# Attention ahead of the MLP with its output kept in DRAM, the last two MLP chunks side by side, and five experts in plain fp32

## Chip, cores and metric

One core of one Trainium2 chip. The metric is the device time of one execution in microseconds (us). Before the change three runs gave 1048.82, 1049.22 and 1049.54 us: a median of 1049.22 us.

## What is computed

Three layers, one after the other, over 4 x 576 = 2304 tokens of width 512. First causal attention with a decay (8 heads of width 64), then an MLP with a squared ReLU, then a layer in which each token goes to one of eight experts, each of which takes 288 tokens.

```python
scores = q @ k.T / 8 + (cum[:, None] - cum[None, :])      # cum = cumsum(log f), causal
x = softmax(scores) @ v                                   # -> (2304, 512)
x = relu(x @ w_in) ** 2 @ w_out                           # 512 -> 2048 -> 512
logits = x @ w_gate                                       # (2304, 8)
# all (token, expert) pairs by falling logit: a token takes the first expert that has room (288)
out[mask_e] = relu(x[mask_e] @ w1[e]) @ w2[e]             # 512 -> 1024 -> 512, e = 0..7
```

## The kernel before

**A recorded program and a planner.** The kernel calls `s.op(...)` for each small task, with the engines that could do it and a cost for each. `Sched.run` then places all tasks by list scheduling: an engine that is free takes the ready task with the lowest `s.base`, from its model of costs. The result is one fixed order for each engine (PE, DVE, ACT, POOL) and for SP, which issues the DMAs. On the chip every engine goes through its own order and stops at an instruction whose inputs are not there.

**Attention** (`attention`, `pair`) goes by batches `b` 0 to 3 and in each by four pairs of heads, 16 pairs in all. A pair has scores on PE (L496), a fused add and minimum on DVE (L513), the exponential on ACT (L520), transposes on PE (L552) with copies out of PSUM, the product with v (L569), and a normalizer: the row sums are transposed on PE (L607), written to DRAM, read back broadcast, and multiplied in (L624, L626). The result of a batch goes to SBUF tiles `xa` (two chunks of 256 tokens) and the first 64 tokens of each batch to `xrem`.

**The MLP** (`moe1_chunk`) goes by nine chunks of 256 tokens: two for each batch, and a last one of the four times 64 tokens in `xrem`. To keep fp32 accuracy at the faster matmul format, operands are split into a high and a low part of type fp32r, and each product is three matmuls. A chunk has 192 first-product matmuls of 256 columns (L692 to L694), then squared ReLU, a split into `hh` and `hl`, and 96 second-product matmuls of 512 columns (L716 to L718). Its 256 output rows go to DRAM (`x2d`), are transposed (L793) and give the logits (L801). The weights, which arrive as 64-bit words, are put together on DVE by three integer instructions for each piece (L656 to L658, 32 pieces) and split, on ACT and POOL above all. All of this is due (`s.base`) in the order: attention 0; weights 1; then for each batch `b` attention `b+1` (2 + 2b) and chunks of `b` (3 + 2b).

**The last chunk** has another form: `gate_weights` works out `w_out @ w_gate` on DVE beforehand (L819), so that the logits come from the hidden layer (L728, L729, then L747), and the second products, which only the gathers need, are due late (29), beside the routing.

**Routing and experts.** `phase(m)` settles which expert fills up next and with which tokens. It is a chain of small DVE instructions with PE between them: three rounds of a histogram (18 matmuls, L1023) with two small matmuls (L1028, L1038) each, then ranks and the list of token numbers (L1119). Phase 7 has no rounds. `expert(m)` then gathers 288 rows of `x2d` (POOL issues three indirect DMAs, L1151), transposes them on PE (L1218), splits them, and does 32 first products as three fp32r matmuls each (L1234 to L1236, 288 columns). The second products (32) are single plain fp32 matmuls (L1259) for experts 0 to 6, and split for expert 7 (L1262 to L1264). A plain matmul has two records in the trace. A split weight is loaded into a tile `wr`; its high part is a copy on ACT, its low part a subtraction on POOL (L1190), 8 pieces of 128 x 512 for each of the two weights. Transposes (L1275), copies, and three indirect DMAs of POOL (L1282) write the result.

```python
PLAIN = range(E - 1)                                                # L44
s.op(lo_alts(512, LOE(m, which, i, 0, c)), ... e.tensor_sub(lo ...  # L1190: POOL for m > 0
```

Of the kernel before, what the change touches and what calls it, by code (L numbers as in the profile page):

```python
# [8 lines left out]
F = mybir.dt.float32  # L9
# [21 lines left out]
XB0 = 1  # L31
RS = [("z", z) for z in (31, 30, 29)]
WS = [("z", 28)]
TM = 1
# [3 lines left out]
NSM = 4  # L38
HM = 50.0
# [4 lines left out]
PLAIN = range(E - 1)  # L44
# [322 lines left out]
class K:  # L367
# [75 lines left out]
    def att_pools(self):  # L443
        self.xp = self.pool("xp", ctx=self.main_es, side="right")
        self.ao = self.pool("ao", ctx=self.att_es)
        self.xrem = self.s.fixed(self.xp.tile([128, 4, 256], F, name="xrem"))
        self.xraw = {}
        self.mark = {}


    def pair(self, b, pr):
# [29 lines left out]
        sums = s.buf(ao, [128, 10], F, "sums", 2)  # L481
        s.op({"pool": 100.0}, lambda e: e.memset(sums.t, 1.0), w=[sums])
# [3 lines left out]
        def scores(parts):  # L486

            sc = [s.buf(self.ps, [128, 512], F, "sc", 2, also=[("u", 0), ("u", 1)] if b == 0 else []) for _ in range(2)]
# [47 lines left out]
        def trans(i, ps_):  # L536
# [22 lines left out]
        def av(g):  # L559
# [12 lines left out]
            xr = self.xraw[b]  # L572
            outs = [(lambda: self.xrem[:, pr, b * 64:b * 64 + 64], 0, 64, [(self.xrem, (b, 2 * pr)), (self.xrem, (b, 2 * pr + 1))])] if g == 0 else []
            outs.append((lambda: xr[g][:, pr, :], n - 256, n, [(xr[g], (pr, 0)), (xr[g], (pr, 1))]))
            for dst, c0, c1, w in outs:
                s.op({"act": act(c1 - c0, True), "dve": dve1(c1 - c0)}, lambda e, dst=dst, c0=c0, c1=c1: self.rnd(e, dst(), ov[:, c0:c1]), r=[ov], w=w)

        return sums, scores, trans, av

    def attention(self, b):  # L580
        self.xraw[b] = [self.s.buf(self.xp, [128, 4, 256], F, "xa", 3) for _ in range(2)][::-1]
        pend = []
        for pr in range(H // 2):
# [9 lines left out]
    def att_tail(self, b, pr, sums, trans, av, i, p):  # L593
# [25 lines left out]
    def norm(self, b, pr, rbc):  # L619
        s = self.s  # L620
        xr = self.xraw[b]
        alts = lambda n: {"dve": dve1(n), "pool": ptt(n)}
        for g in range(2):
            s.op(alts(256), lambda e, g=g: e.tensor_mul(xr[g][:, pr, :], xr[g][:, pr, :], rbc[:, 64 + 256 * g:320 + 256 * g]), r=[rbc],  # L624
                 w=[(xr[g], (pr, j)) for j in range(2)])
        s.op(alts(64), lambda e: e.tensor_mul(self.xrem[:, pr, b * 64:b * 64 + 64], self.xrem[:, pr, b * 64:b * 64 + 64], rbc[:, :64]),  # L626
             r=[rbc], w=[(self.xrem, (b, 2 * pr)), (self.xrem, (b, 2 * pr + 1))])
# [33 lines left out]

    def moe1_chunk(self, b, c):
        s = self.s
        mp = self.mp
        if b < B:
            srcb = self.xraw[b][c]
            keys = lambda k: [(srcb, (k, 0)), (srcb, (k, 1))]
        else:
            srcb = self.xrem
            keys = lambda k: [srcb]  # L670
        xh, xl = [], []
        for k in range(4):
            hh = s.buf(mp, [128, 256], R, f"xh{k}", 1)
            ll = s.buf(mp, [128, 256], R, f"xl{k}", 1)
            s.op(hi_alts(256), lambda e, k=k, hh=hh: self.rnd(e, hh.t, srcb[:, k, :]), r=keys(k), w=[hh])
            s.op(lo_alts(256), lambda e, k=k, hh=hh, ll=ll: e.tensor_sub(ll.t, srcb[:, k, :], hh.t.bitcast(F)), r=keys(k) + [hh], w=[ll])  # L676
            xh.append(hh)
            xl.append(ll)
        final = b == B
        if final:  # L680
            h2 = [[s.buf(self.hp, [128, 4, 256], R, "h2", 5, also=[("xa", i) for i in range(3)]) for _ in range(2)] for _ in range(4)]
        else:
            acc = [s.buf(self.ps, [128, 512], F, "acc", 2) for _ in range(2)]

        def up(f):
            u = s.buf(self.ps, [128, 512], F, "u", 2)
            un = [self.wu[self.unit(0, k, f // 4)] for k in range(4)]
            fs = slice(f % 4 * 128, f % 4 * 128 + 128)
            for k in range(4):
                def g(e, k=k):  # L690
# [703 lines left out]
```

## Time and profile before

| | |
|---|---|
| median of three runs | 1049.22 us |
| the profiled execution | 1047.0 us, its span 1044.9 us |
| PE busy | 951.6 us (91%) |
| DVE busy | 646.0 us (62%) |
| ACT, POOL busy | 413.4 us (40%), 359.6 us (34%) |
| mean granted clock of PE | 0.957 |
| DMA | 96.25 MB, mean 92 GB/s |

The span runs from the first instruction to the last; the profiled execution took 2.1 us more than it. A busy PE is not PE at its peak: records overlap, and a matmul lasts twice as long where the granted clock is 0.5 (1.2 GHz instead of 2.4). So what a product costs is read from the distance between starts, and a stage by what it holds against what it took.

### The profile page before, as it was taken

How to read it: one execution, taken by the hardware profiler on the slowest of the kernel's cores; microseconds unless marked ns; L12 is line 12 of the kernel's file. 1: busy time of each engine (PE TensorE's matmuls, PEld its weight loads, DVE VectorE, ACT ScalarE, POOL GpSimd, SP SyncE). 2: the span in 40 equal slices, each digit the busy share in tenths (PEclk: the TensorE clock that was granted, in tenths of full speed). 3: DMA queues.
4: the chain of work that ended last, by engine and by line, in shares of the span. 5: the costliest groups of instructions: out<-in, count | busy, mean ns of one | idle time of the engine just before them, and what ended most of it. 6: DMA issues, size and time to landing. Idle time of an engine off the chain costs nothing. (4 is left out here: it accounts for less than half of the span.)

```text
span 1044.9 us, 17749 instructions
## 1 busy us (share of the span) xinstructions
PE 951.6 (91%) x6315; PEld 775.2 (74%) x6315; DVE 646.0 (62%) x1951; ACT 413.4 (40%) x1118; POOL 359.6 (34%) x470
## 2 busy tenths in 40 slices
PE   6888899999999999999999999959789778899896
PEld 3555567887778987778988899848678667778785
DVE  6999985305553144457999834568888687842131
ACT  4755555445664455553434344212123123022210
POOL 2667745232213012223334211022561453264521
PEclk9997999999999999999999899969898899899899
DMA  6555542202222002203000000062363254172210
GB/s 207 198 189 184 181 158 82 91 1 81 80 71 90 1 30 85 70 25 112 2 21 1 21 1 22 1 204 65 121 207 122 85 194 174 32 273 67 66 46 24
DMA packets 39977, 96.25 MB, mean 92 GB/s; under 512 B 7784, under 2 KB 12040, under 8 KB 39760
## 3 DMA queue, kind: packets, MB, share of 16 engines
q1 hardware_dynamic: 36816, 85.67, 24.5%
q0 software_dynamic: 3072, 9.44, 3.0%
q8 instruction: 50, 0.82, 0.3%
q14 instruction: 39, 0.32, 0.1%
HBM read 85.48 MB, written 9.61 MB: 91 GB/s over the span
## 5 line engine op out<-in xcount | busy, mean ns | idle before, releaser
L692 PE MATMUL u<-xh,z 128*128 128x256 f32 x576 | 173.9, 302 | 0.7 <-ACT wraw L381 0.5
L694 PE MATMUL u<-xl,z 128*128 128x256 f32 x576 | 164.2, 285 | 0.5 <-POOL xl L676 0.5
L693 PE MATMUL u<-xh,z 128*128 128x256 f32 x576 | 164.1, 285 | 0.0
L1259 PE MATMUL acc<-ehh,z 128*128 128x288 f32 x448 | 132.1, 428 | 1.9 <-ACT ys L381 1.9
L692 PEld LDWEIGHTS u<-xh,z 128*128 128x128 f32 x576 | 110.9, 193 | 22.9 <-issue 11.7
L1190 POOL TENSOR_TENSOR z<-wr,z 128x512 fp32r<-128x512 f32 x64 | 81.3, 1300 | 123.2 <-ACT z L381 117.7
L693 PEld LDWEIGHTS u<-xh,z 128*128 128x128 f32 x576 | 111.2, 193 | 7.4
L697 ACT ACTIVATE r<-u 128x256 f32<-128x256 f32 x144 | 54.4, 380 | 147.3 <-PE u L694 136.4
L694 PEld LDWEIGHTS u<-xl,z 128*128 128x128 f32 x576 | 110.9, 192 | 0.8 <-POOL xl L676 0.8
L819 DVE CUSTOM_DVE_ANT_0 gjk<-wof,wgb 128x512 bf16<-128x512 f32 x128 | 102.8, 803 | 5.9 <-DMA wgb<-wgT 2.3
L718 PE MATMUL acc<-z,hl 128*128 128x512 f32 x256 | 101.1, 395 | 4.1 <-POOL hl L709 2.7
L709 POOL TENSOR_TENSOR hl<-r,hh 128x256 fp32r<-128x256 f32 x79 | 67.3, 854 | 107.5 <-ACT hh L381 89.9
L716 PE MATMUL acc<-z,hh 128*128 128x512 f32 x256 | 102.9, 402 | 1.2 <-POOL hh L383 1.2
L717 PE MATMUL acc<-z,hh 128*128 128x512 f32 x256 | 101.5, 397 | 0.0
L1259 PEld LDWEIGHTS acc<-ehh,z 128*128 128x128 f32 x448 | 81.0, 199 | 23.6 <-issue 6.9
L520 ACT ACTIVATE p<-p,st 128x576 f32<-128x576 f32 (+4 forms) x144 | 79.9, 556 | 45.9 <-DVE st L513 45.2
L513 DVE CUSTOM_DVE_ANT_0 p<-sc,row 128x192 f32<-128x192 f32 (+4 forms) x133 | 60.4, 466 | 45.2 <-PE pt L552 17.1
L1234 PE MATMUL u<-exh,z 128*128 128x288 f32 x216 | 78.5, 363 | 0.0
L508 POOL TENSOR_TENSOR row<-maskb,row 128x128 f32<-128x128 bf16 (+1 forms) x80 | 39.2, 494 | 110.6 <-DVE st L513 86.5
L496 PE MATMUL sc<-qk,qk 64*128 64x512 f32 (+5 forms) x322 | 65.2, 465 | 10.6 <-DMA qk<-in_k_dram 6.1
L1236 PE MATMUL u<-exl,z 128*128 128x288 f32 x216 | 65.3, 302 | 0.0
L1235 PE MATMUL u<-exh,z 128*128 128x288 f32 x216 | 65.3, 302 | 0.0
(346 smaller groups left out, 2030.2 us busy)
## 6 DMA issues: line engine op xcount, KB each, us to landing
wr<-in_w_dram SPq DMA_DIRECT2D x32, 512.0 KB
z<-in_w_dram SPq DMA_DIRECT2D x28, 512.0 KB
z<-in_w_in_dram SPq DMA_DIRECT2D x16, 512.0 KB
row<-cumd SPq DMA_DIRECT2D x28, 288.0 KB
z<-in_w_out_dram SPq DMA_DIRECT2D x14, 512.0 KB
vr<-in_v_dram SPq DMA_DIRECT2D x14, 320.0 KB
qk<-in_q_dram SPq DMA_DIRECT2D x15, 288.0 KB
wraw<-rd SPq DMA_DIRECT2D x32, 128.0 KB
```

The source lines that it names most:

```text
L520: s.op({"act": act(w, extra=2)}, lambda e, x=x, si=si, i=i, n=n, w=w, p=p[x], st=st[x]: e.activation(p[:n, :w], p[:n, :w], AF.Exp, bias=st ...
L692: e.matmul(u[:, :256], wh[:, k % 2, fs], xh[k].t, start=(k == 0), stop=False)
L693: e.matmul(u[:, :256], wl[:, k % 2, fs], xh[k].t, start=False, stop=False)
L694: e.matmul(u[:, :256], wh[:, k % 2, fs], xl[k].t, start=False, stop=(k == 3))
L709: s.op(lo_alts(256), lambda e: e.tensor_sub(hl(), r.t, hh().bitcast(F)), r=[r, kh], w=[kl])
L716: g = [lambda e, t=t, ts=ts: e.matmul(acc[t].t, hh()[:, ts], wh[:, f % 2], start=(f == 0), stop=False), lambda e, t=t, ts=ts: e.matmul(acc ...
L717: lambda e, t=t, ts=ts: e.matmul(acc[t].t, hh()[:, ts], wl[:, f % 2], start=False, stop=False),
L718: lambda e, t=t, ts=ts: e.matmul(acc[t].t, hl()[:, ts], wh[:, f % 2], start=False, stop=(f == 15))]
L819: s.op({"dve": dve1(DM) + 85}, lambda e, f=f, x=x, wo=wo, jk=jk: e.tensor_tensor_reduce(out=jk.t, in0=wo.t, in1=wb[:, x, :], scale=1.0, sc ...
L1190: s.op(lo_alts(512, LOE(m, which, i, 0, c)), lambda e, cs=cs: e.tensor_sub(lo[:, cs], raw[:, cs], hi[:, cs].bitcast(F)), r=[(raw, key), (h ...
L1234: e.matmul(u[:, :CAP], whi[0][k][:, fs], xh[k].t, start=(k == 0), stop=False)
L1259: e.matmul(acc[:, :CAP], wh[:, ds], hh.t, start=(f == 0), stop=(f == 7))
```

## The change

1. **Attention ahead.** All four batches come before the chunks in the recording, due at 0, 0.5, 0.6 and 2, the weights at 1, the chunks at 3, 5, 7 and 9. Attention's output (`xo`, 128 x 576 for each pair) is written to a DRAM tensor `xd` after its normalization, and each chunk reads its 256 tokens back (`moe1_x`). The tiles that attention borrows from the weights' place and from the MLP's PSUM are lent to batches 0 to 2, not to batch 0 alone (`XB0`, `XB1`).
2. **The last two chunks side by side** (`moe1_last`): chunk (3, 0) and the one of the 4 x 64 tokens are done together. Both get their logits from the hidden layer, and the second products of both are due late. The hidden layer lies in the places of first-product weights that are used up. Routing's first part takes the first 12 row tiles, the second the last 6, where it was 16 and 2.
3. **Five plain experts**: experts 0 to 4 do both products as plain fp32 matmuls, with weights loaded straight into their places; experts 5 to 7 do both split. The planner's cost of a plain product goes from 1.89 to 1.69 ns a column.

```diff
-XB0 = 1
+XB0 = 3
+XB1 = 3
+ABASE = (0, 0.5, 0.6, 2)
-PLAIN = range(E - 1)
+PLAIN = (range(5), range(5))
...
-        self.xrem = self.s.fixed(self.xp.tile([128, 4, 256], F, name="xrem"))
+        self.xd = self.s.fixed(self.dr.tile([B, 4, 128, S], F, name="xd"))
...
+        xo = s.buf(self.xp, [128, S], F, "xo", 2)
...
+            s.op({"act": act(n, True), "dve": dve1(n)}, lambda e: self.rnd(e, xo[:, base:base + n], ov[:, :n]), r=[ov], w=[(xo, g)])
...
+        self.dma(lambda: self.xd[b, pr], lambda: xo.t, 128 * S * 4, r=[xo], w=[(self.xd, (b, pr))])
...
+    def moe1_x(self, b, c, two=False):
+        srcb = s.buf(self.xp, [128, 4, 256], F, "xa", 3)
+        for i in [b] if b < B else range(B):
+            dst, c0, n = (slice(0, 256), 64 + 256 * c, 256) if b < B else (slice(64 * i, 64 * i + 64), 0, 64)
+            self.dma(lambda dst=dst: srcb[:, :, dst], lambda i=i, c0=c0, n=n: self.xd[i, :, :, c0:c0 + n].rearrange("k p s -> p k s"),
+                     512 * n * 4, r=[(self.xd, (i, j)) for j in range(4)], w=[(srcb, i)])
...
+    def moe1_last(self, chunks):
+        xs = [self.moe1_x(b, c, two=i > 0) for i, (b, c) in enumerate(chunks)]
...
+        for f in range(16):
+            prev.append([self.moe1_up(f, *xs[i], h2=h2[f // 4][i]) for i in range(n)])
+            if f >= 1:
+                for i in range(n):
+                    gate(f - 1, i)
...
+        for i, (b, c) in enumerate(chunks):
             s.base = 29
             acc = [s.buf(self.ps, [128, 512], F, "acc", 2) for _ in range(2)]
+            for t in range(2):
                 for f in range(16):
+                    self.moe1_down(f, t, acc[t], *prev[f][i], one=False)
...
-            parts = [slice(0, 16), slice(16, 18)] if m == 0 else [slice(0, 18)]
+            parts = [slice(0, 12), slice(12, 18)] if m == 0 else [slice(0, 18)]
...
-        plain = m in PLAIN
+        plain = [m in x for x in PLAIN]
...
+                if plain[0]:
+                    s.op({"pe": 1.69 * CAP}, lambda e, k=k: e.matmul(u[:, :CAP], whi[0][k][:, fs], xh[k].t, start=(k == 0), stop=(k == 3)), r=[(whi[0][k], c), xh[k]], w=[u])
+                    continue
...
-    k.attention(0)
+    for b in range(B):
+        s.base = ABASE[b]
+        k.attention(b)
...
-        if b + 1 < B:
-            s.base = 2 + 2 * b
-            k.attention(b + 1)
...
-        for c in (1, 0):
+        for c in (1, 0) if b + 1 < B else (1,):
             k.moe1_chunk(b, c)
...
-    k.moe1_chunk(B, 0)
+    k.moe1_last([(B - 1, 0), (B, 0)])
```

**What moves on PE in the opening.** Before: PE's order near the normalizer of the fourth pair (L607); first products of chunk 0 (`u`, L692 to L694) already stand between instructions of attention, and 15 of them stand before it.

```order
L569 MATMUL ov_916<-pb_831,z_631 64x128
L552 MATMUL pt_944<-ident,p_887 64x64
L552 MATMUL pt_944<-ident,p_897 64x64
L692 MATMUL u_873<-xh_932,z_483 128x256
L693 MATMUL u_873<-xh_932,z_500 128x256
L694 MATMUL u_873<-xl_936,z_483 128x256
L692 MATMUL u_881<-xh_736,z_310 128x256
L693 MATMUL u_881<-xh_736,z_340 128x256
L694 MATMUL u_881<-xl_746,z_310 128x256
L607 MATMUL pt_959<-ident,sums_605 10x128
```

After the change, PE's order around the first of them (now L691 to L693; scores are L499, transposes L555, products with v L572, the normalizer L605):

```order
L572 MATMUL ov_2346<-pa_2269,vr_2003 64x128
L555 MATMUL pt_2368<-ident,z_2271 128x128 x4
L555 MATMUL acc_2369<-ident,z_2292 128x128 x4
L555 MATMUL ov_2384<-ident,z_2271 128x128
L555 MATMUL ov_2384<-ident,z_2292 128x128
L691 MATMUL u_2390<-xh_1231,z_310 128x256
L692 MATMUL u_2390<-xh_1231,z_340 128x256
L693 MATMUL u_2390<-xl_1256,z_310 128x256
L691 MATMUL u_2390<-xh_1236,z_310 128x256
L692 MATMUL u_2390<-xh_1236,z_340 128x256
L693 MATMUL u_2390<-xl_1294,z_310 128x256
L555 MATMUL pt_2404<-ident,p_2306 128x128 x4
```

They stand behind the normalizer of the eleventh pair; before the normalizer of pair 13 there are 81 first and 30 second products.

**What moves on PE at the routing.** Before: the end of phase 0. Behind the last second product (`acc`, L716 to L718) come the list of phase 0 (L1119; L1135 there is a sum for the next phase) and, behind that, phase 1 with nothing beside it.

```order
L1078 MATMUL ov_7775<-ph_M_7963,rc_pre 128x36
L1080 LDWEIGHTS rc_ones_5580
L1080 MATMUL ov_7775<-ph_M_7963,rc_ones_5580 128x36
L716 MATMUL acc_7360<-z_1809,xa_7657 128x512
L717 MATMUL acc_7360<-z_1820,xa_7657 128x512
L718 MATMUL acc_7360<-z_1809,xa_7662 128x512
L1135 LDWEIGHTS ph_c_8013
L1135 MATMUL ov_7775<-rc_ones_5580,ph_c_8013 128x2
L1119 LDWEIGHTS ph_OH_8029
L1119 MATMUL sc_8036<-ph_gi_8025,ph_OH_8029 96x6
```

After the change, in phase 1: the two small matmuls of its first round (L1044, L1054) stand between second products (L715 to L717).

```order
L715 MATMUL acc_7783<-z_2484,z_7322 128x512
L716 MATMUL acc_7916<-z_1509,z_7154 128x512
L716 MATMUL acc_7783<-z_2539,z_7322 128x512
L1044 MATMUL ov_7682<-ph_h_8040,rc_tri 128x2
L717 MATMUL acc_7783<-z_2484,z_7327 128x512
L717 MATMUL acc_7916<-z_1501,z_7159 128x512
L715 MATMUL acc_7783<-z_2484,z_7322 128x512
L715 MATMUL acc_7916<-z_1501,z_7154 128x512
L716 MATMUL acc_7783<-z_2539,z_7322 128x512
L1054 LDWEIGHTS rc_ones_3773
L1054 MATMUL ov_7682<-ph_PB_8054,rc_ones_3773 128x8
```

Of the 192 second products of the last two chunks 69 stand between the lists of phase 0 and phase 1; the first transposes of gathered rows follow the list of phase 1.

**What moves on POOL.** Before: between the DMAs that write an expert's rows (L1282) and those that gather the next one's (L1151) stand the subtractions that make low parts of weights (L1190).

```order
L1282 DMA out_dram<-yo_8625,ph_idx_8085 2304x512
L1190 TENSOR_TENSOR z_9035<-wr_8914,z_9004 128x512 x2
L1151 DMA xg_9082<-x2d,ph_idx_9075 96x512 x3
L1190 TENSOR_TENSOR z_9125<-wr_8925,z_9058 128x512 x2
L1190 TENSOR_TENSOR z_9143<-wr_8934,z_9086 128x512 x2
L1190 TENSOR_TENSOR z_9174<-wr_8947,z_9102 128x512 x2
L1190 TENSOR_TENSOR z_9464<-wr_9359,z_9435 128x512
L1281 MEMSET spacer_8794 1x1
```

After the change, the gathers of experts 0, 1 and 2 and the first row write of expert 0 (L1306); nothing but gathers and writes follows up to the gather of expert 4:

```order
L1167 DMA xg_8266<-x2d,ph_idx_7991 96x512 x3
L1167 DMA xg_8527<-x2d,ph_idx_8345 96x512 x3
L1167 DMA xg_8758<-x2d,ph_idx_8752 96x512 x3
L1305 MEMSET spacer_9219 1x1
L1306 DMA out_dram<-yo_8813,ph_idx_7991 2304x512
```

The first subtractions (now L1206, eight of them for expert 5) stand behind that gather, in phases 5 and 6.

## Rows read from the trace of the kernel before

**Rows 1.** Busy time by stage: us, then PE, PEld, DVE, ACT, POOL busy (count), PE clock, DMA
```profile
0.00:169.60 169.60, 144.24 (x870) 94.41 (x871) 149.57 (x391) 95.40 (x283) 94.18 (x139) 0.94 0.56 181
169.60:664.00 494.40, 488.51 (x3292) 406.80 (x3290) 264.21 (x751) 242.70 (x672) 122.50 (x190) 0.99 0.13 44
...
688.10:728.70 40.60, 29.78 (x213) 26.69 (x214) 29.79 (x110) 7.49 (x17) 12.09 (x8) 0.75 0.40 131
728.70:767.00 38.30, 31.67 (x232) 27.05 (x231) 32.55 (x112) 9.32 (x21) 18.00 (x17) 0.91 0.43 145
...
879.10:916.40 37.30, 30.60 (x218) 25.66 (x217) 31.23 (x106) 6.54 (x14) 13.79 (x11) 0.91 0.36 128
...
921.00:1044.90 123.90, 109.60 (x669) 96.31 (x667) 30.58 (x68) 21.59 (x47) 50.45 (x60) 0.95 0.26 81
```

**Rows 2.** Timeline of PE: normalizers of pairs 1, 6 and 7 (start us, us, engine, line)
```profile
29.86 0.28 PE L607 MATMUL pt<-ident,sums 128*10 128x128 f32 x1 [0.31 <-DVE pa L385]
...
143.15 0.27 PE L607 MATMUL pt<-ident,sums 128*10 128x128 f32 x1
...
169.63 0.27 PE L607 MATMUL pt<-ident,sums 128*10 128x128 f32 x1
```

**Rows 3.** Groups of DVE instructions: the weight pieces (xcount, busy us, mean ns, idle before)
```profile
L657 DVE SCALAR_TENSOR_TENSOR wa<-z,wa 128x512 uint32<-128x512 uint32 x16 | 14.2, 887 | 0.1
L658 DVE SCALAR_TENSOR_TENSOR wa<-z,wa 128x512 uint32<-128x512 uint32 x16 | 14.1, 879 | 0.1
...
L656 DVE TENSOR_SCALAR wa<-z 128x512 uint32<-128x512 uint32 x16 | 9.3, 583 | 0.0
```

**Rows 4.** Windows with PE at the lower clock in the opening (columns as in Rows 1)
```profile
77.00:91.00 14.00, 10.52 (x38) 7.14 (x39) 13.90 (x27) 7.49 (x20) 9.83 (x11) 0.51 0.59 179
```

**Rows 5.** Timeline of PE: the transposes at the ends of three chunks
```profile
241.91 0.64 PE L793 MATMUL u<-ident,wraw 128*128 128x128 f32 x4
...
333.94 1.09 PE L793 MATMUL u<-ident,wraw 128*128 128x128 f32 x8
...
384.00 0.66 PE L793 MATMUL u<-ident,wraw 128*128 128x128 f32 x4
```

**Rows 6.** Timeline of PE: starts from which the price of one product is read
```profile
659.73 0.28 PE L692 MATMUL u<-xh,z 128*128 128x256 f32 x1
659.85 0.28 PE L693 MATMUL u<-xh,z 128*128 128x256 f32 x1
...
664.89 0.63 PE L716 MATMUL acc<-z,h 128*128 128x512 f32 x2
665.36 0.63 PE L717 MATMUL acc<-z,h 128*128 128x512 f32 x2
...
923.39 3.10 PE L1259 MATMUL acc<-ehh,z 128*128 128x288 f32 x12
926.12 0.51 PE L1234 MATMUL u<-exh,z 128*128 128x288 f32 x1
...
941.61 0.29 PE L1234 MATMUL u<-exh,z 128*128 128x288 f32 x1
...
942.00 0.29 PE L1234 MATMUL u<-exh,z 128*128 128x288 f32 x1
```

**Rows 7.** Timeline: DVE beside runs of POOL in the routing, and the next PE gap
```profile
739.45 6.16 POOL L1190 TENSOR_TENSOR z<-wr,z 128x512 fp32r<-128x512 f32 x5
...
739.68 5.97 DVE L997 TENSOR_SCALAR ph_ti<-ph_P,ph_th 128x18 int32<-128x18 f32 x1
...
747.22 0.80 PE L1023 MATMUL ov<-ph_G,ph_OH 128*128 128x128 bf16 x6 [3.54 <-DVE ph_G L1012]
...
889.92 6.32 DVE L997 TENSOR_SCALAR ph_ti<-ph_P,ph_th 128x18 int32<-128x18 f32 x1
```

**Rows 8.** Timeline of PE: the first transpose of gathered rows
```profile
701.87 0.42 PE L1218 MATMUL pt<-ident,xg 96*128 96x96 f32 x1 [6.04 <-DMA xg<-x2d,ph_idx]
```

**Rows 9.** Groups of POOL instructions: the gathers (xcount, busy us, mean ns, idle before)
```profile
L1151 POOL DMA_INDIRECT xg<-x2d,ph_idx x24 | 29.9, 1244 | 12.1 <-issue 8.4 <-DMA z<-in_w_dram 1.6 <-DVE ph_idx L1125 1.5
```

More of the change, by code (lines that the diff above doesn't have):

```diff
@@ new lines, in moe1_down @@
+    def moe1_down(self, f, t, acc, hh, hl, kh, kl, one=True):
+        s = self.s
+        wh, wl = self.wu[self.unit(1, f, 0)]
+        ts = slice(t * 128, t * 128 + 128)
+        g = [lambda e: e.matmul(acc.t, hh()[:, ts], wh[:, f % 2], start=(f == 0), stop=False),
+             lambda e: e.matmul(acc.t, hh()[:, ts], wl[:, f % 2], start=False, stop=False),
+             lambda e: e.matmul(acc.t, hl()[:, ts], wh[:, f % 2], start=False, stop=(f == 15))]
+        r = [kh, kl, (wh, f % 2), (wl, f % 2)]
+        if one:
+            s.op({"pe": mm(512, 3)}, lambda e: [x(e) for x in g], r=r, w=[acc])
+        else:
+            for x in g:
+                s.op({"pe": mm(512)}, x, r=r, w=[acc])
@@ L662, in moe1_chunk @@
     def moe1_chunk(self, b, c):
         s = self.s
[L664 to L678, printed above, removed]
@@ L726, in gate, with down @@
-        def gate(f, hh, hl, kh, kl):
+        xh, xl = self.moe1_x(b, c)
+        acc = [s.buf(self.ps, [128, 512], F, "acc", 2) for _ in range(2)]
+        def down(f):
+            for t in range(2):
+                self.moe1_down(f, t, acc[t], *prev[f])
+        prev = []
+        for f in range(16):
+            prev.append(self.moe1_up(f, xh, xl))
+            if f >= 2:
+                down(f - 2)
+        down(14)
+        down(15)
+        for t in range(2):
+            self.x2_tail(b, c, t, acc[t])
@@ new lines, in moe1_last, with gate @@
+    def moe1_last(self, chunks):
+        s = self.s
+        xs = [self.moe1_x(b, c, two=i > 0) for i, (b, c) in enumerate(chunks)]
+        n = len(chunks)
+        hz = [("z", 2 * t + x) for t in range(16) if t % 4 < 2 and t < 12 for x in range(2)]
+        h2 = [[[s.buf(self.hp, [128, 4, 256], R, "h2", 4, also=hz) for _ in range(2)] for _ in range(n)] for _ in range(4)]
+        pl = [s.buf(self.ps, [128, 512], F, "plg", 0, also=[("sc", 0), ("sc", 1)]) for _ in range(n)]
+        def gate(f, i):
+            hh, hl, kh, kl = prev[f][i]
@@ L760, in moe1_chunk @@
                 self.x2_rows(b, c, t, acc[t])
[L761 to L770 removed]
+        self.x2_done = s.tasks[-3]
     def x2_rows(self, b, c, t, acc):
@@ L1164, in wload @@
             us = [t for t in range(16) if (t % 4 >= 2) == which]
-            if which and plain:
-                wt = s.buf(self.wp, [128, 1024], F, "w1p", 0, also=[("z", 2 * t + x) for x in range(2) for t in us])
+            if plain[which]:
+                wt = s.buf(self.wp, [128, 1024], F, f"w{which}p", 0, also=[("z", 2 * t + x) for x in range(2) for t in us])
                 whi[which].append(wt)
```

188 lines of the change are left out of this document (82 added, 106 removed).

## Prediction

> **What bounds the kernel now.** I read the busy time by stage first. The stages are cut at marks in PE's timeline: the normalizer of pair 7 (169.6 [rows 2]), the first logits of the last chunk (664.0, L747), and the token lists of the phases (L1119, from 688.1 to 921.0) [rows 1]. Three regimes show. From 169.6 to 664.0 PE is busy 488.5 of 494.4 us at clock 0.99: PE is the bound, and only the number of products and their price count. In the opening PE is busy 144 of 169.6 and DVE 150, and in the lower-clock window of the opening DVE has 13.90 of 14.00 us [rows 4]. There DVE is the bound: it makes the pairs' minima and the weight pieces. In the routing no engine is full (a phase of 38.3 us has 31.7 of PE and 32.6 of DVE, at clock 0.91), so a chain of waits is the bound. The end from 921.0 is PE's again, at 109.6 of 123.9.
>
> The profiled execution took 1047.0 us: a span of 1044.9 and 2.1 around it. The median of the runs is 2.2 above it. I work in the span and add 4.3 at the end.
>
> **Prices.** A weight piece costs DVE 0.583 + 0.887 + 0.879 = 2.35 us [rows 3]. From the normalizer of pair 1 to that of pair 6 there are 143.15 - 29.86 = 113.3 us [rows 2]; DVE's order has 28 of the 32 pieces there, 65.8 us, which leaves (113.3 - 65.8) / 5 = 9.5 us of DVE for each pair. For PE, one chunk alone takes 384.00 - 333.94 = 50.1 us, one with four pairs beside it 333.94 - 241.91 = 92.0 [rows 5]: 10.5 us of PE for a pair. A first-product matmul costs 0.12 us from start to start, a second-product one 0.47 for two, 0.235. An expert's product costs 2.73 / 6 = 0.455 plain (twelve records are six products) and 942.00 - 941.61 = 0.39 as three matmuls [rows 6].
>
> **A, the opening, up to the normalizer of pair 13.** Attention now runs with no chunk beside it up to pair 11. DVE's order has 29.5 pieces between the normalizers of pairs 1 and 13. With the start as before, pair 13 is done at 29.9 + 12 x 9.5 + 29.5 x 2.35 = 213. Before, the same time bought pair 7 and about 43 us of chunks. Bounds: 205 (a few pieces in DVE's idle time) and 235 (DVE waits for PE in part).
>
> **B, from there to the first logits of the last chunks.** PE is full here, so I count against the 494.4 us that followed pair 7. Three pairs are left where nine were: -6 x 10.5 = -63.0. The order has done 81 first products where it had 180, so 99 more are left: +11.9. It defers 164 second products past the first logits where it deferred 76, and has done 30 where it had 78, so 40 fewer stand in this stretch: -9.4. The transposes and logits of one chunk go: -2.7, an estimate from the 0.66 us for four transposes [rows 5] and as much for the logits. Thirty logit products at the price of a first product come: +3.5. Together -59.7: 434.7 us, so 647.7 where it was 664.0. Bounds: 640 and 664.
>
> The DMAs that come with it are 16 writes of 0.29 MB, one for each pair, and the reads of the same 4.7 MB. They stand on SP's queue. A read could be late at the start of a chunk, for which the nearest row is the 6.04 us that PE waited for a gather [rows 8]; against it stands that the order puts all four writes of a batch at least one batch before the first read of it. The DMA engines have room for them, at 0.56 and 0.13 of their time [rows 1]. I take 0, with 0 to 6 us once.
>
> **C, the first logits to the list of phase 1.** Before it was 24.1 + 40.6 = 64.7 us. In the second part nothing stood beside phase 1: PE's clock was 0.75, and PE waited 6.04 us for the gather [rows 1, 8]. Now 95 second products stand in the first part and 69 in the second, so PE has 26.8 and 20.4 us of work for them by the prices. The chain of phase 1 runs at full clock, but each of its small matmuls queues behind a second product. I take 60.5, between 57 (only PE's gaps go) and 65 (nothing goes).
>
> **D, the list of phase 1 to that of phase 7.** Before 921.0 - 728.7 = 192.3 us, of which five phases of 37.5 on the mean; PE's work by the prices is 26.9 in each. The timeline shows why they are longer. An instruction of 18 columns on DVE (L997) lasts 5.97 us: it starts while POOL is in a run of subtractions, 6.16 us for five, ends with that run, and PE then sits idle for 3.54 us [rows 7]. The same happens once in every phase, with 5.97 us in the first of five and 6.32 in the last, 29.0 together [rows 7]. The plain experts 0 to 4 have no low parts, so these runs go from POOL's order until those of expert 5. I take the stalls out: 37.5 - 5.8 = 31.7, and 0.8 back of the 1.6 us by which the plain first products of a phase are dearer: 32.5. The floor is PE's 28.5. The first of the five has the gather's wait in it, as before some 6 us and 2 more for what now lies between the last second product and the gather: 34. Sum: 34 + 4 x 32.5 + 5 (one run for expert 5) + 4.6 (phase 7) = 173.6. Bounds: 165 and 192.
>
> The Trainium skill says otherwise of such stalls ("SBUF — State Buffer", section "Who interferes with whom"): DVE and GpSimd share one port pair under an exclusive lock, and whoever issues first holds it for its whole instruction, the other engine being blocked. By that, DVE would wait for one subtraction and not for the run; the rows here show waits of the whole run.
>
> **E, the end.** The list of phase 7 is followed by 221 products now and by 273 after the change, because three experts instead of one do both products split and the phases ahead are shorter; by the prices 102 and 124 us. Before, 123.9 were taken for 102. I take 20 of those 21.9 us of waits and clock again: 144. Bounds: 136 (half of the gap) and 156 (below).
>
> **Sum.** 213 + 434.7 + 60.5 + 173.6 + 144 = 1025.8 against 1044.9: A and B together give 16, C 4, D 19, and E takes 20 back. With the 4.3 us this is **1030 us** on the runs' median. The gain of the plain experts is a moved cost in part: PE pays 5 x 32 x 0.065 = 10.4 us more for the plain first products and gets 2 x 32 x 0.065 = 4.2 back from experts 5 and 6.
>
> **The rivals.**
> *1, the lower clock in attention (slower).* Up to pair 11 PE has only 10.5 us of work for a pair, in 9.5 + 2.46 x 2.35 = 15.3 us of DVE's. PE was like that from 77 to 91: busy 10.5 of 14, the clock at 0.51, the lower of the two levels [rows 4]. At that level a pair takes PE 21 us, 5.7 more than DVE, and PE becomes the bound. The gain of 18 us is used up by 3.2 such pairs; with six of twelve the time is 1030 + 34 = 1064. For it: no chunk fills PE's gaps any more. Against it: at 0.51 DVE was still full in that row, and a PE that is the bound has no gaps. Chance 0.12.
> *2, the stalls are shorter than the rows suggest.* Then POOL's runs were beside the point, except for one subtraction of 1.23 us in each phase. The phases would be 37.5 - 1.2 = 36.3, which gives 1030 + 4 x 3.8 = 1045, or 1055 if all stays and PE pays the dearer products. Against it: five of five stalls end with the run. This is what the port lock of the Trainium skill would make of it, and the rows so far speak against that. Chance 0.10.
> *3, POOL in the end.* Three experts with both products split give POOL 16 x 1.23 = 19.7 us of subtractions each, 3.7 for the gather (1.244 each [rows 9]) and about as much for the row writes, 27 in all against PE's 25 for 64 products. A gather then stands behind the subtractions of the expert before, and each expert waits some 4 us: +12, which is E's upper bound, 1042. Chance 0.12.
> *4, nearer the floors.* DVE's idle time takes some pieces (-8) and the phases come down to 29.5 (-12): 1010. Chance 0.08.
>
> **How the numbers follow.** The forecast has 0.58, its own range being 1014 to 1045. With rivals 2 to 4 the range is 1008 to 1056; left out are rival 1 and half of rival 4, and a few parts of the rest. A measurement of this kernel tells 0.2% (2.1 us) from no change, so faster means below 1047.1. The forecast gives 0.54 to that, rivals 4 and 3 give 0.08 and 0.09, and rival 2 gives 0.03: 0.74. Slower is rival 1 with 0.12, and the upper ends of the forecast, of rival 2 and of rival 3 with 0.02 each: 0.18. Same is the rest: 0.08.
>
> **What would show it.** Right: the normalizer of pair 13 near 213 with DVE full before it; the first logits near 648; L997 short in phases 2 to 5, with phases near 32.5; some 144 us after the last list. Wrong: long stretches at clock 0.5 with PE full before pair 11; phases of 36 us and more without POOL beside them; gathers in the end that start late behind L1206.

## The result, and the profile after

The changed kernel takes 1010.39 us (median of 4 runs, 1008.18 to 1012.48) where the kernel before took 1049.02 (4 runs): a ratio of 0.9636, interval 0.9609 to 0.9662. The forecast was 1030, its range 1008 to 1056. The sign and the range held; the gain is 38.6 us where 19 were forecast.

The stages of the changed kernel, cut at the same marks as [rows 1]: the normalizer of pair 13 (217.0), the first logits of the last two chunks (643.6), and the lists of phases 0 to 7 (670.2 to 868.4). The columns are those of [rows 1].

```profile
0.00:217.00 217.00, 186.09 (x1242) 112.32 (x1242) 192.12 (x599) 133.03 (x411) 114.93 (x192) 0.94 0.67 216
217.00:643.60 426.60, 422.03 (x2833) 370.38 (x2833) 212.92 (x536) 197.25 (x521) 93.25 (x128) 0.99 0.10 33
643.60:670.20 26.60, 26.60 (x155) 19.77 (x155) 18.42 (x96) 1.19 (x2) 0.15 (x1) 1.00 0.10 36
670.20:697.50 27.30, 21.23 (x153) 16.97 (x152) 19.88 (x99) 0.60 (x1) 1.50 (x2) 0.92 0.20 51
697.50:732.70 35.20, 28.75 (x177) 23.20 (x178) 22.51 (x106) 3.77 (x10) 5.38 (x5) 0.77 0.79 257
732.70:762.80 30.10, 30.10 (x198) 23.93 (x197) 22.19 (x104) 1.99 (x5) 4.41 (x4) 1.00 0.50 173
762.80:794.30 31.50, 30.47 (x202) 24.14 (x201) 22.58 (x104) 3.91 (x10) 8.16 (x9) 1.00 0.48 165
794.30:824.70 30.40, 30.33 (x196) 23.88 (x194) 22.38 (x108) 4.80 (x12) 5.83 (x8) 1.00 0.46 159
824.70:862.10 37.40, 33.01 (x196) 25.39 (x194) 28.18 (x101) 7.81 (x16) 13.03 (x12) 0.91 0.31 100
862.10:868.40 6.30, 5.62 (x40) 4.33 (x41) 4.12 (x20) 0.90 (x2) 1.30 (x3) 1.00 0.37 126
868.40:1009.40 141.00, 128.37 (x850) 116.83 (x848) 34.79 (x77) 38.56 (x84) 73.38 (x79) 0.98 0.30 94
```

Against the terms of the sum, in the span:

| term | forecast | measured | difference |
|---|---|---|---|
| A, to the normalizer of pair 13 | 213 | 217.0 | +4.0 |
| B, to the first logits | 434.7 | 426.6 | -8.1 |
| C, to the list of phase 1 | 60.5 | 53.9 | -6.6 |
| D, to the list of phase 7 | 173.6 | 170.9 | -2.7 |
| E, to the end | 144 | 141.0 | -3.0 |
| from the span to the runs' median | 4.3 | 1.0 | -3.3 |

C is 26.6 + 27.3, D the six rows behind it. The phases without POOL's subtractions (732.7 to 824.7) take 30.1 to 31.5 us with PE full. The long DVE instructions are gone: the groups of the instruction that [rows 7] show, of the kernel before and, under its new line, of the changed one (xcount, busy us, mean ns):

```profile
L997 DVE TENSOR_SCALAR ph_ti<-ph_P,ph_th 128x18 int32<-128x18 f32 x14 | 22.7, 1621 | 0.5
```

```profile
L1013 DVE TENSOR_SCALAR ph_ti<-ph_P,ph_th 128x18 int32<-128x18 f32 x14 | 3.3, 236 | 0.5
```

In the end PE is busy 128.4 of 141.0 us where it was 109.6 of 123.9 [rows 1].

### The profile page after: what moved, and what is told of

Same layout as the page of the kernel before. It is cut to its first block, busy times and chain, and to the rows that moved or that the text cites. A ratio compares the mean times of both kernels' runs of the same rounds, so it can differ in the third digit from the quotient of the medians.

```text
span 1009.4 us, 17558 instructions
## 1 busy us (share of the span) xinstructions
PE 942.6 (93%) x6231; PEld 761.1 (75%) x6231; DVE 600.1 (59%) x1941; ACT 393.8 (39%) x1072; POOL 321.3 (32%) x439
## 5 line engine op out<-in xcount | busy, mean ns | idle before, releaser
L691 PE MATMUL u<-xh,z 128*128 128x256 f32 x512 | 148.9, 291 | 2.3 <-ACT r L696 1.9
L692 PE MATMUL u<-xh,z 128*128 128x256 f32 x512 | 145.6, 284 | 0.0
L693 PE MATMUL u<-xl,z 128*128 128x256 f32 x512 | 145.4, 284 | 0.0
L691 PEld LDWEIGHTS u<-xh,z 128*128 128x128 f32 x512 | 98.1, 192 | 15.4 <-issue 3.1
L692 PEld LDWEIGHTS u<-xh,z 128*128 128x128 f32 x512 | 98.3, 192 | 8.1
L693 PEld LDWEIGHTS u<-xl,z 128*128 128x128 f32 x512 | 98.2, 192 | 0.0
L1283 PE MATMUL acc<-ehh,z 128*128 128x288 f32 x320 | 92.1, 421 | 0.0
L717 PE MATMUL acc<-z,hl 128*128 128x512 f32 x224 | 89.2, 398 | 1.9 <-POOL hl L708 1.6
L715 PE MATMUL acc<-z,hh 128*128 128x512 f32 x224 | 90.9, 406 | 0.0
L716 PE MATMUL acc<-z,hh 128*128 128x512 f32 x224 | 89.7, 400 | 0.0
L1254 PE MATMUL u<-exh,z 128*128 128x288 f32 x304 | 86.5, 420 | 0.1
L1206 POOL TENSOR_TENSOR z<-wr,z 128x512 fp32r<-128x512 f32 x48 | 61.1, 1305 | 48.0 <-ACT z L383 47.9
L523 ACT ACTIVATE p<-p,st 128x448 f32<-128x448 f32 (+4 forms) x109 | 59.9, 550 | 38.0 <-DVE st L516 36.2
L1283 PEld LDWEIGHTS acc<-ehh,z 128*128 128x128 f32 x320 | 57.5, 194 | 15.9 <-issue 1.6
L1254 PEld LDWEIGHTS u<-exh,z 128*128 128x128 f32 x304 | 55.5, 194 | 14.6 <-DVE exh L387 0.3
L697 ACT ACTIVATE r<-r 128x256 f32<-128x256 f32 x138 | 57.6, 418 | 4.1
L1167 POOL DMA_INDIRECT xg<-x2d,ph_idx x24 | 25.6, 1069 | 98.6 <-DVE ph_P L1109 51.9
```

The lines of the kernel that those rows point to most:

```text
L523: s.op({"act": act(w, extra=2)}, lambda e, x=x, si=si, i=i, n=n, w=w, p=p[x], st=st[x]: e.activation(p[:n, :w], p[:n, :w], AF.Exp, bias=st ...
L691: e.matmul(u[:, :256], wh[:, k % 2, fs], xh[k][1](), start=(k == 0), stop=False)
L692: e.matmul(u[:, :256], wl[:, k % 2, fs], xh[k][1](), start=False, stop=False)
L693: e.matmul(u[:, :256], wh[:, k % 2, fs], xl[k][1](), start=False, stop=(k == 3))
L715: g = [lambda e: e.matmul(acc.t, hh()[:, ts], wh[:, f % 2], start=(f == 0), stop=False), lambda e: e.matmul(acc.t, hh()[:, ts], wl[:, f % ...
L716: lambda e: e.matmul(acc.t, hh()[:, ts], wl[:, f % 2], start=False, stop=False),
```

## The experiments

Each ratio is to the kernel before, timed beside that run; so ratios, and not times, are compared between runs.

**The parts one by one.** Four runs undo one part each, or spread the second products otherwise; two leave one part alone.

*Plain experts undone*:

```diff
-PLAIN = (range(5), range(5))
+PLAIN = (range(0), range(7))
```

> The changed kernel with the experts' formats of the kernel before: first products split for all eight, second products plain for experts 0 to 6. Theory (POOL's runs of subtractions hold DVE up in the phases): phases 2 to 6 go back towards 37.5 us, some 24 us more between the lists of phase 1 and 7; PE's work falls by 6 us; time 1024 to 1032, and L1013 or L1053 of several us at the end of a POOL run shows in several phases. Rival (the phases became shorter through other parts of the change): phases stay at 30 to 32 us and PE's work falls by 6 us; time 1003 to 1008.

Measured: 1039.71 us, 0.9921 (0.9897 to 0.9945). Phases 2 to 6 are back at 34.7 to 40.9 us, and so are the holds, DVE instructions that last as long as a run of POOL's subtractions beside them. The stretches of phases 3 and 5, and two of the holds in the timeline:

```profile
739.80:777.00 37.20, 32.29 (x237) 27.83 (x235) 31.79 (x109) 6.90 (x15) 15.14 (x11) 0.95 0.37 127
...
811.70:852.60 40.90, 34.68 (x222) 28.60 (x221) 32.76 (x107) 8.27 (x19) 16.82 (x18) 0.87 0.40 138
```

```profile
750.60 6.21 POOL L1206 TENSOR_TENSOR z<-wr,z 128x512 fp32r<-128x512 f32 x5
...
751.33 5.52 DVE L1013 TENSOR_SCALAR ph_ti<-ph_P,ph_th 128x18 int32<-128x18 f32 x1
...
875.18 7.41 POOL L1206 TENSOR_TENSOR z<-wr,z 128x512 fp32r<-128x512 f32 x6
...
876.67 5.96 DVE L1053 TENSOR_SCALAR ph_PB<-rc_blk,ph_cnt 128x8 bf16<-128x8 f32 x1
```

The theory holds, and is too small: 2.9% by the ratios, some 30 us, where it gave 14 to 22. Two holds took other instructions than the ones named (L1007 for 6.82 us, L1025 for 4.59).

*Last chunk alone* (with routing's parts of 16 and 2 again):

```diff
-        for c in (1, 0) if b + 1 < B else (1,):
+        for c in (1, 0):
...
-    k.moe1_last([(B - 1, 0), (B, 0)])
+    k.moe1_last([(B, 0)])
```

> The changed kernel with the last chunk alone at the end, as before (76 second products due late, none beside phase 1); attention ahead and five plain experts stay. Theory 1 (second products beside phase 1 fill time that is idle otherwise): the list of phase 0 to that of phase 1 goes from 27.3 to about 40 us at a lower clock, of which PE's work of expert 0 fills a part; time 1018 to 1024. Theory 2 (the idle time is only moved: without second products there expert 0's own products stand in phase 1, and the wait for the first gather falls from phase 2): time 1008 to 1014.

Measured: 1013.88 us, 0.9692 (0.9645 to 0.9739). Phase 1 goes to 41.4 us at clock 0.75 (theory 1), yet little is lost (theory 2): phase 2 takes 29.3 instead of 35.2, the end 115.2 instead of 141.0. And one new thing: phase 6 takes 45.9 us. Phases 1, 2 and 6 and the end:

```profile
684.00:725.40 41.40, 30.83 (x172) 23.86 (x173) 23.06 (x107) 1.97 (x5) 4.83 (x3) 0.75 0.44 136
725.40:754.70 29.30, 29.30 (x198) 23.53 (x197) 23.73 (x108) 2.69 (x6) 7.37 (x9) 1.00 0.54 179
844.50:890.40 45.90, 32.02 (x196) 25.22 (x195) 40.25 (x105) 10.61 (x21) 24.31 (x19) 0.89 0.32 102
895.30:1010.50 115.20, 103.09 (x739) 97.36 (x737) 30.24 (x67) 33.57 (x75) 60.97 (x68) 0.97 0.30 92
```

In phase 6 DVE's instruction of 18 columns is held for 14.31 us, behind expert 5's gathers:

```profile
853.13 0.92 POOL L1167 DMA_INDIRECT xg<-x2d,ph_idx  x1 [0.30 <-issue]
...
854.07 14.76 POOL L1206 TENSOR_TENSOR z<-wr,z 128x512 fp32r<-128x512 f32 x12
...
854.56 14.31 DVE L1013 TENSOR_SCALAR ph_ti<-ph_P,ph_th 128x18 int32<-128x18 f32 x1
...
870.44 1.74 PE L1039 MATMUL ov<-ph_G,ph_OH 128*128 128x128 bf16 x12 [11.64 <-DVE ph_G L1028]
```

*Attention beside the chunks again* (`XB0` and `XB1` back to 1):

```diff
-ABASE = (0, 0.5, 0.6, 2)
+ABASE = (0, 2, 4, 6)
```

> The changed kernel with attention of batch b due beside the chunks of batch b-1 again, and the borrowed places lent to batch 0 alone; its output still goes through memory, the last two chunks are side by side, five plain experts. Theory (in the opening and the middle the time up to the first logits fell by 20.4 us, of which 88 second products that are deferred account for 20.7, so the earlier attention by itself gave nothing): first logits within 5 us of 643.6, time 1006 to 1016. Rival (attention ahead gains in the opening because DVE is kept full): first logits 10 to 20 us later, time 1020 to 1030.

Measured: 1026.06 us, 0.979 (0.9744 to 0.9836). The first logits come at 666.0, 22.4 us later: the rival's time, but not its reason alone. PE waits 14.92 us for gate weights, because two chunks side by side want them a chunk earlier, and DVE makes them from 489.9 us on, behind the last pair (from 300.3 in the changed kernel). From the first logits on this run is 7.7 us shorter than the changed kernel: phase 6 takes 28.7 us, with none of expert 5's subtractions in it, and the end 149.5. The wait:

```profile
613.49 0.37 PE L757 MATMUL sc<-h,g 128*16 128x256 f32 x1 [14.92 <-DVE g L840]
```

*Second products early* (in `moe1_last`):

```diff
-            s.base = 29
+            s.base = 11
```

> The changed kernel with the second products of the last two chunks due early: all 164 that are left at the first logits stand ahead of the list of phase 0 and none beside phase 1. Theory 1 (they fill idle time in phase 1): first logits to the list of phase 1 goes from 53.9 to about 80 us and the rest gets 10 to 15 us shorter; time 1018 to 1026. Theory 2 (only moved): time 1008 to 1014.

Measured: 1032.05 us, 0.9851 (0.98 to 0.9902): slower than either theory. The two parts of C take 53.1 and 41.8 us, the second at clock 0.74. That is 94.9 instead of 53.9 with the same 164 second products in it: the first part is longer by 26.5, of which the 69 products moved there are 16 by their price, and the second by 14.5 though they are gone from it. What follows is 22.5 us shorter. The hold in phase 6 is 16.68 us here, beside 14 subtractions:

```profile
869.48 17.14 POOL L1206 TENSOR_TENSOR z<-wr,z 128x512 fp32r<-128x512 f32 x14
...
869.98 16.68 DVE L1013 TENSOR_SCALAR ph_ti<-ph_P,ph_th 128x18 int32<-128x18 f32 x1
```

*Five plain experts alone* (the edits of the second and third run together):

> Of the three parts only the five plain experts stand: attention beside the chunks and the last chunk alone, as before (attention's output still goes through memory). Theory (POOL's runs were most of the routing's excess): lists of phase 1 to 6 some 30 us apart as in the run with the last chunk alone, unless expert 5's run of subtractions meets DVE, which costs some 14 us once; time 1015 to 1030. Rival (plain experts pay only together with the other parts): 1040 to 1050.

Measured: 1027.21 us, 0.982 (0.9784 to 0.9856), with a hold of 14.35 us in phase 6 and phases 2 to 5 at 29.4 to 30.8. First logits at 672.5, 8.5 us behind the 664.0 of the kernel before. Up to there the two differ by the way of attention's output through memory above all, but no run shows that this is the cause.

*Attention ahead alone* (the edits of the first and second run together):

> Of the three parts only attention ahead stands. Theory (attention ahead by itself gives nothing; the 22 us that it was worth in the run that undid it came from gate weights that were late for two chunks side by side, a gap of 14.9 us on PE before the first logit product, and from the clock behind it): first logits within 5 us of 664, time 1040 to 1050. Rival (it gains by itself): first logits near 645, time 1020 to 1030.

Measured: 1040.02 us, 0.9936 (0.9913 to 0.9958). First logits at 659.2, 4.8 us earlier than in the kernel before with the same products done. One trace is thin for a difference of this size: in the eight traces with attention ahead, five or four plain experts and the last chunk alone the first logits come at 658.9 to 663.7, in the two with the order of the kernel before at 664.0 and 665.1. Phases 2 to 6 take 37.3 to 39.0 us.

**What holds DVE.** All holds over 2 us up to here lay beside a run of subtractions that stood directly behind an indirect DMA of POOL; where POOL had waited for ACT's copy first, DVE was held for one subtraction. So the next runs took POOL's run away, and tried waits in four places.

*Expert 5's low parts on DVE* (last chunk alone):

```diff
-LOE = lambda m,w,i,j,c: "dve pool" if m==0 else "pool"
+LOE = lambda m,w,i,j,c: "dve pool" if m==0 else "dve" if m==5 else "pool"
```

> The run with the last chunk alone (attention ahead, five plain experts), with expert 5's low parts made on DVE instead of POOL. Theory (a run of POOL's subtractions directly behind its gathers held a DVE instruction of 18 columns for 14.3 us in phase 6): phase 6 goes from 45.9 to 32 to 35 us, time 999 to 1005. Rival (the stall has another cause, or DVE's sixteen subtractions cost the chain as much): 1010 to 1018.

Measured: 1001.25 us, 0.9564 (0.9537 to 0.9591). Phase 6 and the end (the next run has the rows of the same):

```profile
847.30:879.80 32.50, 32.40 (x206) 25.27 (x205) 28.42 (x113) 12.92 (x29) 3.43 (x3) 1.00 0.44 142
886.00:1000.80 114.80, 103.23 (x728) 98.03 (x728) 30.53 (x66) 30.49 (x67) 58.24 (x66) 0.95 0.29 92
```

*Copies between the subtractions*: on ACT, one element of each result of POOL to a tile of its own.

> The run with the last chunk alone, with a one-element copy on ACT between any two of expert 5's subtractions on POOL: POOL's run gets a short wait behind each subtraction, and its work and place stay. Theory (DVE is held as long as POOL goes from one instruction to the next without a wait): the DVE instruction waits for one subtraction, at most 2 us, and phase 6 is 32 to 36 us; time 1000 to 1006. Rival (DVE waits for the last subtraction in any case): 14 us and more remain; time 1012 to 1020.

Measured: 1012.75 us, 0.9672 (0.964 to 0.9705). The edit did not do what was meant: no subtraction reads a copy, so none waits for one, and POOL's starts stay 1.25 us apart. The hold was 9.45 us beside 8 subtractions. It tells nothing of a wait.

*A wait behind the gathers*, in the kernel before, in the run with the last chunk alone, and with attention ahead alone; and the same without a wait:

```diff
+                    if g == 2:
+                        e.tensor_copy(self.spacer.t, xg[0:1, 2, 0:1])      # or: e.memset(self.spacer.t, 0.0)
```

> The kernel before, with a copy of one element of the gathered rows on POOL behind the third gather of each expert, so that POOL waits until the rows are there before it goes on to its subtractions. Theory (in all traces a DVE instruction was held for a whole run of subtractions only where the run stood directly behind an indirect DMA of POOL; behind a wait of POOL it was held for one): the five stalls of 3.3 to 7.8 us become 1.3 us each at most, phases 2 to 6 come to 31 to 34 us; time 1022 to 1032. Rival 1 (the length of the run decides, whatever is ahead of it): stalls and time as before, 1045 to 1052. Rival 2 (POOL's low parts are now late): DVE is free, but PE waits for subtractions; 1040 to 1050.

Measured: 1039.21 us, 0.9942 (0.992 to 0.9963). Four DVE instructions still last over 2 us: 2.58, 7.41 (to the end of a run of seven subtractions), 2.17 and 6.72, in phases 3 to 6. The two phases with the long ones take 38.5 and 38.6 us, the three others 32.4 to 33.4: with formats and products as they were, the phases come down where the long hold goes.

> The run with the last chunk alone, with the same copy behind the gathers of every expert. Theory (the run directly behind the gather held DVE for 14.3 us): the stall goes to 1.3 us, phase 6 from 45.9 to 31 to 35 us; time 999 to 1005, as where expert 5's low parts were made on DVE. Rival (the run's length decides): 14 us and 1010 to 1018.

Measured: 1018.28 us, 0.9748 (0.9711 to 0.9784). POOL waited 2.51 us, and the run behind it held DVE for 15.27 us all the same:

```profile
854.38 0.27 POOL L1170 COPY spacer<-xg 1x1 f32<-1x1 f32 x1 [2.51 <-DMA xg<-x2d,ph_idx]
854.53 15.27 DVE L1028 TENSOR_TENSOR ph_G<-ph_bb,rc_i 128x768 bf16<-128x768 bf16 x1
854.63 14.76 POOL L1208 TENSOR_TENSOR z<-wr,z 128x512 fp32r<-128x512 f32 x12
```

> The run with the last chunk alone, with a one-element memset on POOL directly behind the third gather and no wait for the rows. Theory 1 (POOL must have waited, another instruction between does not help): the stall of some 14 us stays; time 1010 to 1018. Theory 2 (only the place directly behind the indirect DMA matters): the stall goes; 999 to 1005.

Measured: 1014.15 us, 0.9711 (0.9677 to 0.9744); hold 14.38 us.

> The run with attention ahead alone (the experts' formats of the kernel before, last chunk alone), with the copy behind the gathers. Theory (as for the kernel before): of its five long stalls behind gathers 30 us go, those behind row writes stay; phases 2 to 6 from 38 to 32 to 34 us; time 1008 to 1022. Rival: 1036 to 1044.

Measured: 1034.84 us, 0.9883 (0.9845 to 0.9922). Three holds of 7.3 to 7.9 us stay, two of them behind the copy. So the theory that the indirect DMA ahead of the run decides has fallen.

*A wait between any two subtractions*: ACT's next copy into `hi` waits for POOL's result, and POOL for that copy.

```diff
+                        if last:
+                            e.activation(hi[0:1, cs.start:cs.start + 1], last[0][0:1, 512 * last[1]:512 * last[1] + 1].bitcast(F), AF.Copy)
                         self.rnd(e, hi[:, cs], raw[:, cs])
```

> The run with the last chunk alone; for expert 5 each copy on ACT that makes a high part is put behind the subtraction before it (it first writes one element read from that subtraction's result), so that POOL must wait between any two subtractions, behind its gathers too. Theory (DVE is held as long as POOL goes from one instruction to the next without a wait): no DVE instruction is held over 2 us, phase 6 goes from 45.9 to 32 to 38 us; time 999 to 1008. Rival (DVE is held until the last subtraction of the expert): a hold of 14 us or more stays; time 1012 to 1025.

Measured: 1005.86 us, 0.9599 (0.9581 to 0.9617), phase 6 at 36.0 us. POOL waits 0.97 us ahead of each subtraction, though the first one again follows the gathers at once, and DVE is held for one at a time:

```profile
850.98 0.92 POOL L1168 DMA_INDIRECT xg<-x2d,ph_idx  x1 [0.30 <-issue]
...
851.92 1.29 POOL L1215 TENSOR_TENSOR z<-wr,z 128x512 fp32r<-128x512 f32 x1
...
854.16 1.35 DVE L1014 TENSOR_SCALAR ph_ti<-ph_P,ph_th 128x18 int32<-128x18 f32 x1
854.18 1.30 POOL L1215 TENSOR_TENSOR z<-wr,z 128x512 fp32r<-128x512 f32 x1 [0.97 <-ACT z L384]
...
856.45 1.28 POOL L1215 TENSOR_TENSOR z<-wr,z 128x512 fp32r<-128x512 f32 x1 [0.97 <-ACT z L384]
856.48 1.67 DVE L1029 TENSOR_TENSOR ph_G<-ph_bb,rc_i 128x768 bf16<-128x768 bf16 x1
```

**Versions with lower ratios.**

*The changed kernel with expert 5's low parts on DVE*:

> The changed kernel with expert 5's low parts made on DVE. Theory (phase 6 of the changed kernel, 37.4 us where phases 3 to 5 take 30 to 31.5, is long through POOL's subtractions): phase 6 at 31 to 33 us; time 1003 to 1007. Rival (phase 6 is long for want of rows or work): 1009 to 1012.

Measured: 1001.93 us, 0.9573 (0.9519 to 0.9627). Phase 6 takes 31.8 us instead of 37.4; sixteen subtractions cost DVE 10.2 us:

```profile
824.10:855.90 31.80, 31.73 (x204) 25.08 (x203) 25.18 (x107) 9.02 (x20) 2.20 (x5) 1.00 0.39 124
861.20:1001.30 140.10, 127.73 (x842) 116.25 (x840) 39.22 (x84) 38.84 (x85) 62.30 (x70) 0.97 0.30 95
```

*Experts 6 and 7 on DVE or POOL as well* (last chunk alone):

> The run with the last chunk alone and expert 5's low parts on DVE, with those of experts 6 and 7 on DVE or POOL as the planner finds (in the end DVE is idle three quarters of the time). Theory (the end waits for POOL here and there: 114.8 us for 98.3 of PE's work by the prices): the end is 3 to 8 us shorter; time 993 to 999. Rival (the end is PE's): 999 to 1003.

Measured: 1001.32 us, 0.9559 (0.9525 to 0.9593). The end takes 114.1 us with 34.0 of POOL, where it took 114.8 with 58.2: it is PE's, not POOL's.

```profile
884.10:998.20 114.10, 101.65 (x728) 95.64 (x728) 43.87 (x83) 31.37 (x71) 33.97 (x45) 0.97 0.29 92
```

*Four plain experts* (last chunk alone, low parts of 4 and 5 on DVE):

> The run with the last chunk alone and expert 5's low parts on DVE, with expert 4 split as well and its low parts on DVE: PE's work falls by 4.2 us by the prices, DVE gets sixteen subtractions more in phases 5 and 6. Theory (PE sets the phases, DVE has room): time 997 to 1000. Rival (DVE's chain sets the phases, each subtraction is in its way): 1002 to 1010.

Measured: 1000.36 us, 0.9549 (0.9533 to 0.9565). The end falls to 102.7 us, and phases 5 and 6 rise to 36.3 and 37.3, since part of the work moved there; phase 7 has a hold of 5.11 us behind a row write. In time it is no difference that the intervals can tell from the two before. All four versions lie 0.6 to 0.9% below the changed kernel by their ratios; the intervals of the three with the last chunk alone lie below its own (0.9609 to 0.9662), that of the other meets it.

## Why the prediction was right in sign and half as large as the gain

What bounds each stage came as the prediction has it; the steps that failed are sizes, in B that of attention ahead and in C the queue behind second products. The sum came out 19.7 us too high (1030.1 for 1010.4), of which B's 434.7 (measured 426.6) and C's 60.5 (53.9) are 14.7; the step from the span to the median, E and D are 9.0 more, and A takes 4.0 back.

**A held.** DVE paces the opening (busy for 192 of 217 us), as the sum had it; pair 13 came 4 us late. Rival 1 came for a moment only: from 120 to 130 us the clock was 0.68, with PE full and DVE busy for 7.36 of 10, but over the opening it was 0.94, as in [rows 1].

**B was mis-sized by 8.1 us**, above all in the step "so 99 more are left: +11.9", which counts first products at 0.12 wherever they stand. Counted from each start on PE to the next with waits left out, the first products of B took 194.9 us before (1548, 0.126 each) and 201.9 after (1647, 0.123 each): +7.0, 4.9 less than the step. The step "Three pairs are left where nine were: -6 x 10.5 = -63.0" came out: all that is not a product, a transpose or a logit of the MLP went from 97.0 to 33.5 us, -63.5. The transposes and logits (-0.9 instead of +0.8) and PE's waits (5.9 to 4.6) are most of the rest.

What the sum had wrong here is attention ahead. In A and B together the forecast took 19.9 us off for the last two chunks (88 second products deferred, -20.7; transposes -2.7; logits +3.5) and 16.3 in all, so it charged 3.6 us to attention ahead. The run with attention ahead alone shows a gain of 4.8 us: 8.4 off, of which the last two chunks, worth 15.6 (659.2 to 643.6), take 4.3 back. Where the gain comes from, counted in the same way: all 1728 first products take 222.9 us in the kernel before and 211.2 in the run with the last chunk alone. In the kernel before one costs 0.205 us on the mean behind another instruction than a product of the MLP, attention's mostly (119 of them), and 0.121 between two products of the MLP (1536); in the other run 52 stand so. The clock is a small part: 18 stood in the window of [rows 4] and took 4.3 us, 2.1 more than at 0.12. Attention's transposes, now without chunks between them, give 7.1 of it back (53.1 to 60.2).

**C was mis-sized by 6.6 us**, in the step "each of its small matmuls queues behind a second product. I take 60.5". With 26.8 for the first part, that left 33.7 for the second, which took 27.3 with 69 second products in it. (At 0.235 the 95 and 69 second products are 22.3 and 16.2 us; the prediction does not say what the rest of its 26.8 and 20.4 is.) The chain of phase 1 is not slowed by them: the three rounds of its histogram start at 675.36, 682.66 and 689.51, some 7 us apart. Where none stand beside it, phase 1 takes 41.4 and 41.8 us at clock 0.75 and 0.74, as two runs show, and the trace of the run with the last chunk alone says why. There the transposes of expert 0's rows stand between the chain's matmuls on PE, the chain waits for the gather with them, and the second round comes 21.1 us behind the first:

```profile
686.96 2.67 PE L1039 MATMUL ov<-ph_G,ph_OH 128*128 128x128 bf16 x18 [1.73 <-DVE ph_G L1028]
...
697.26 0.42 PE L1234 MATMUL pt<-ident,xg 96*128 96x96 f32 x1 [7.63 <-DMA xg<-x2d,ph_idx]
...
708.09 1.20 PE L1039 MATMUL ov<-ph_G,ph_OH 128*128 128x128 bf16 x18
```

In the sum a part of these waits stayed (its lowest C was 57); with expert 0's transposes behind the list of phase 1 they are gone.

**D's mechanism is shown.** Forecast and measured differ by 2.7 us, from the phases without POOL (30.1 to 31.5 instead of 32.5; the 1.6 us for dearer products there is 2.1 by the prediction's own 32 x 0.065). Phase 6 with expert 5's subtractions was put at 37.5 and took 37.4, but that is luck in part: the sum had one long hold there, and the trace has five DVE instructions of 1.23 to 1.62 us in turn with POOL, the first and the third of them here:

```profile
825.85 2.91 POOL L1206 TENSOR_TENSOR z<-wr,z 128x512 fp32r<-128x512 f32 x2 [3.10 <-ACT z L383]
826.15 1.49 DVE L1025 TENSOR_TENSOR ph_OH<-rc_i,ph_q 128x768 bf16<-128x768 bf16 x1
...
829.23 5.84 POOL L1206 TENSOR_TENSOR z<-wr,z 128x512 fp32r<-128x512 f32 x4 [0.47 <-ACT z L383]
829.57 1.62 DVE L1025 TENSOR_TENSOR ph_OH<-rc_i,ph_q 128x768 bf16<-128x768 bf16 x1
```

Undoing the plain experts brings the holds back, and 30 us; taking expert 5's run off POOL shortens phase 6 from 37.4 to 31.8 us; and waits between the subtractions end the long hold. Rival 2 is out, and with it the forecast by the rule of the Trainium skill ("SBUF — State Buffer", "Who interferes with whom"), by which a hold is one instruction long.

**E** was put 3.0 us too high, at PE's work plus 20 of waits; PE worked 128.4 of 141.0. Rival 3 is out: in the version with the last chunk alone the end stayed as long when much of POOL's work was taken off (114.8 and 114.1 us). **The step from the span to the median** put 2.2 us on top because the profiled run of the kernel before lay that much below its median; here span and median differ by 1.0.

**The parts are not worth what their stages show.** By ratios, the plain experts take off 1.8% alone (with attention's output through memory) and 2.9% as the last part; attention ahead 0.6% alone and 1.5% as the last part, of which the late gate weights are a share. Two chunks side by side take 11 us out of C (64.6 and 53.8 us in the versions with expert 5 on DVE), but with the holds gone the two versions, one chunk or two, are equal (0.9564 and 0.9573): phase 2 gives 6 us back to the wait for the gather, which now comes behind the last second product, and the end has the products that phase 1 no longer did.

## What to carry to other kernels

A small instruction that lasts as long as a neighbour's whole run of work is a hold, and the fix is to move that run or break it with waits: expert 5's subtractions on DVE cost it 10 us of its time and made phase 6 shorter by 5.6 us or, with the last chunk alone, by 13. Price a product where it stands: the same first products cost 5% less in sum with attention out of their way. And judge a part with the others in place: filling 11 us of waits gave nothing, since the work put there was missing later.

## What the runs showed of the hardware that was not expected

DVE was held beside back-to-back POOL subtractions of 1.25 us for 14.31 us (12 of them) and 16.68 us (14); instructions of 8 and of 768 columns were held as one of 18 is (7.41 and 15.27 us the longest). With 0.97 us of wait between them it was held for one (1.35 us). The Trainium skill's rule on the shared port pair ("SBUF — State Buffer", "Who interferes with whom") says that the lock is held for the whole instruction; the paced run agrees, the others do not, and the measurement decides. But there are also runs without such waits in which the two engines took turns (in the changed kernel DVE has four instructions of 1.49 to 1.62 us and one of 1.23 beside expert 5's first two runs, of two and four subtractions). There POOL waits too, and this is a sign of it in a trace: in all traces, from the list of phase 0 on, a subtraction that took 1.34 us or more beside a DVE instruction, with another subtraction right behind it, was followed by DVE's turn (23 of 23); of those that DVE waited past, none took over 1.32. What decides between the two was not found: neither the indirect DMA ahead of the run, nor a wait ahead of it, nor a memset.
